# Attention and two MLPs on one core: an earlier start, a lower rank and a longer planned landing for the second MLP's weight narrowing

## The chip, the core and the metric

The kernel runs on one core of a Trainium2 chip. The metric is the device time of one execution in microseconds (us); of the kernel before there are three runs, and their median stands below. One further execution was taken with the hardware profiler, and all rows come from that one.

## The reference

```python
# attention with a window of 64 over 4 batches, 8 heads, 576 positions, 64 per head
scores = scale * np.matmul(q, k.transpose(0, 1, 3, 2))
scores = np.where((rel >= 0) & (rel < 64), scores, -1000000000.0)
attn = softmax(scores); x = attn @ v        # 2304 tokens x 512
# first MLP, 512 -> 2048 -> 512
h = x @ w_in
x = (h * (1.0 / (1.0 + np.exp(-1.702 * h)))) @ w_out
# second MLP, 512 -> 1536 -> 512
xn = x / np.sqrt(np.mean(x * x, axis=-1, keepdims=True) + 1e-06) * rms_g
g = xn @ w_gate
out = (g * (1.0 / (1.0 + np.exp(-g))) * (xn @ w_val)) @ w_out
```

All five weight matrices arrive as float64, so every weight is narrowed to float32 on the chip from its bits, and the products are made of a high and a low part of each operand (three matmuls for one).

## The kernel before, in words

**Stages.** The tokens are cut into 36 groups of 64 for the attention and into six blocks of 512, 256 and four times 384 tokens for the first MLP. The first eight groups are done at the start. Then the first MLP runs as 96 steps, 16 for each block (step s = 16 x block + column): 12 matmuls of an up-projection (L554 to L556), a gate on ScalarE and VectorE (L607, L611, L312, L569), and two steps later 12 matmuls of a down-projection (L628 to L630). The attention of the next block's groups runs beside the steps. When a block is finished, its sums of squares go through a small chain of DMAs to DRAM and back: `ms` (L706), `ss` (L697), a root on GpSimd (L693), and the store `rs` (L700) of four-byte words. After step 95 the second MLP runs on three blocks of 768 tokens (L912 to L914, L1013 to L1015).

**One round of attention.** Scores (L428, TensorE), mask and highest (L453, L458, VectorE), powers (L463, ScalarE), reciprocal (L468, L469, VectorE), normalisation (L472, GpSimd), a turn of the tile (L477 on TensorE up to the second block; after it L520 on VectorE with some ten small moves into the tile `pts` on ScalarE and GpSimd, L312 and L314), then the values (L487, TensorE). The loads are `q` (L398), `k` (L405) and `v` (L413), all on SP's queue. The tiles `q` and `k` have two buffers; `v` has one, so that the load for the next round is issued only after L487 of this one.

**Narrowing a second-MLP weight.** There are 36 of them (12 tiles each of gate, value and out). `b_narrow` calls `w_narrow`, which loads 512 KB of float64 into one of three `raw` buffers (L336, SP), scales the high words (L340, ScalarE), and shifts, joins and signs on VectorE (L344, L348, L354). For a pair of gate or value tiles four sums follow (L1172, VectorE or GpSimd), and each half of the pair is stored to DRAM (`wp`, L1175, 512 KB); its buffer is free for the next raw load only when that store has landed. An out tile is signed into a `y` buffer, so its raw buffer is free at once, and it is stored with L1158 (`wr`). The second MLP later reads these stores back (`fw`, L865, and L898).

**What sets the order.** Nothing of this order is decided on the chip. `Planner` holds every operation with a cost, its dependencies and a rank (`prio`), and `emit` plays the program through in planned time: of the operations that are ready, the one with the lowest rank number goes first, and each engine's instructions are then written out in that order. Each engine, SP's queue among them, runs its list strictly in order. A DMA counts as landed a planned 2.2 us after its transfer, plus `late`:

```python
if best == "D" or o.late:
    o.end += self.DMA_WAIT + o.late
```

So `late` costs no time on the chip by itself: it only makes the planner place what uses the data further back. Weight i of the 36 is planned around step `p = n0 + i * (n1 - n0) / 36`, and its load is not issued before the up-projection of step p - 2.

Of the kernel before, what the change touches and what calls it, by code (L numbers as in the profile page):

```python
# [11 lines left out]
I32 = mybir.dt.int32  # L12
# [5 lines left out]
P = 128  # L18
# [171 lines left out]
def act(n, sbuf=True, extra=0):  # L190
    return n / 1200.0 + (0.093 if sbuf else 0.05) + 0.093 * extra


def dve(n, fast=False):
    return n * (0.52e-3 if fast else 1.042e-3) + 0.068


def pool(n):
    return n * 2.4e-3 + 0.16


def dma(nbytes):
    return max(nbytes / 320e3, 0.45)
# [3 lines left out]
def window_attention_two_moe_kernel(ctx: ExitStack, tc: tile.TileContext, ins, out):  # L207
    nc = tc.nc
# [14 lines left out]
    NBA = len(sizes)  # L223
# [66 lines left out]
    pl = Planner({k: v[1] for k, v in KINDS.items()})  # L290
# [5 lines left out]
    def make(b):  # L296
        if b.kind == "pt":
            b.tile = pts
            return pts
        if b.kind == "xa":  # L300
            turn = xa_turn[0] = 1 - xa_turn[0]
            b.tile = words(SUMS)[:, turn * 512:(turn + 1) * 512].rearrange("p (k c) -> p k c", k=NK)
            return b.tile
        p, n, shape, dt = KINDS[b.kind]
        b.tile = p.tile(shape, b.dt or dt, tag=b.kind, name=b.kind, bufs=n)
        return b.tile
# [21 lines left out]

    w32 = {}

    def w_narrow(key, src, prio, after=(), apart=False):
        rb = Buf("raw")
        fb = Buf("y") if apart else rb

        def fetch(e):
            nc.sync.dma_start(out=make(rb), in_=src.bitcast(I32).rearrange("p (n two) -> p n two", two=2))  # L336

        def scaled(e):
            high = rb.tile[:, :, 1].bitcast(F32)
            nc.scalar.activation(out=high, in_=high, func=AF.Copy, scale=2.0 ** -112)  # L340

        def shifted(e):
            low = rb.tile[:, :, 0]
            nc.vector.tensor_scalar(out=low, in0=low, scalar1=29, scalar2=None, op0=ALU.logical_shift_right)  # L344

        def joined(e):
            low, high = rb.tile[:, :, 0], rb.tile[:, :, 1]
            nc.vector.scalar_tensor_tensor(  # L348
                out=low, in0=high, scalar=3, in1=low, op0=ALU.logical_shift_left, op1=ALU.bitwise_or)

        def signed(e):
            low, high = rb.tile[:, :, 0], rb.tile[:, :, 1]
            to = make(fb).bitcast(I32) if apart else high
            nc.vector.scalar_tensor_tensor(  # L354
                out=to, in0=high, scalar=-2147483648, in1=low, op0=ALU.bitwise_and, op1=ALU.bitwise_or)

        got = pl.op({"D": dma(P * 4096)}, fetch, prio - 3, new=[rb], after=after, late=5.0 if apart else 0.0)
        pl.op({"A": act(512)}, scaled, prio, w=[rb])
        pl.op({"V": dve(512, True)}, shifted, prio, w=[(rb, "low")], after=[got], port="V")
        pl.op({"V": dve(512)}, joined, prio, w=[rb], r=[(rb, "low")], port="V")  # L360
        if apart:
            pl.op({"V": dve(512)}, signed, prio, r=[rb, "at"], new=[fb], port="V")
        else:
            pl.op({"V": dve(512)}, signed, prio, r=["at"], w=[rb], port="V")
        w32[key] = fb
# [235 lines left out]
    def a_up(j, c, prio):  # L601
        n = sizes[j]
        hb, o = up("h", lambda: slab_of(2 * c), ("slab", 2 * c), tok0[j], n, prio)
        tb = Buf("th")

        def squash(e):
            nc.scalar.activation(out=make(tb)[:, 0:n], in_=hb.tile[:, 0:n], func=AF.Tanh, scale=0.851)  # L607

        def gated(e):
            th = tb.tile[:, 0:n]  # L610
            nc.vector.scalar_tensor_tensor(out=th, in0=th, scalar=1.0, in1=hb.tile[:, 0:n],  # L611
                                           op0=ALU.add, op1=ALU.mult)

        pl.op({"A": act(n, False)}, squash, prio, r=[hb], new=[tb])
        pl.op({"V": dve(n)}, gated, prio, r=[hb], w=[tb])
        return split(tb, n, prio, tok0[j]), o
# [128 lines left out]
    def both(n, alone=False):  # L745
        return {"V": dve(n)} if alone else {"G": pool(n), "V": dve(n)}
# [96 lines left out]
    w32p_d = [dr_p.tile([P, 2, 512, 2], F32, name=f"wp{n}") for n in range(NU)]  # L843
    w32o_d = [dr_p.tile([P, 512], F32, name=f"wr{c}") for c in range(NB)]
# [238 lines left out]
    for g in range(NS):  # L1083
        late = g >= 2
# [13 lines left out]
    first, need = {}, {}  # L1098
# [7 lines left out]
    for i in order:  # L1106
        c = i // 2
        key, src = (("in", c), w_in[c]) if i % 2 == 0 else (("out", c), w_out[c])
        prio = need[i] - LEAD if need[i] > 0 else -57.5
        w_narrow(key, src, prio)  # L1110
        w_split(key, i, prio)
# [10 lines left out]
    ups = []  # L1122
# [15 lines left out]
        b_list.append((("v", c), w_val[c], c - c % 2 + 1))  # L1138
        b_list.append((("o", c), w_o2[c], c + 2))
    b_list.sort(key=lambda x: x[2])  # L1140
    n0, n1 = first[2] + 2, first[NBA - 1] - 4

    def ex_open(e):
        actx.close()
# [6 lines left out]
    def b_narrow(i):  # L1151
        (kind, c), src, _ = b_list[i]
        p = n0 + i * (n1 - n0) / len(b_list)
        key = ("w32d", "o", c) if kind == "o" else ("w32d", c - c % 2 + "gv".index(kind), c % 2)
        w_narrow(key, src, p + 3, after=[ups[int(p) - 2]], apart=kind == "o")
        b = w32.pop(key)
        if kind == "o":
            pl.op({"D": dma(P * 2048)}, lambda e: nc.sync.dma_start(out=w32o_d[c], in_=b.tile), p + 3, r=[b], w=[key])  # L1158
            return
        n = key[1]  # L1160
        if c % 2 == 0:
            halfway[n] = b
            return
        pair = (halfway.pop(n), b)

        def word(h, k, lane):
            return pair[h].tile[:, k * 256:(k + 1) * 256, lane].bitcast(F32)

        for to, x, y, op in (((0, 0), (1, 0, 1), (1, 1, 1), ALU.add), ((0, 1), (0, 0, 0), (0, 0, 1), ALU.subtract),
                             ((1, 0), (0, 0, 1), (1, 0, 1), ALU.subtract), ((1, 1), (0, 1, 1), (0, 1, 0), ALU.subtract)):  # L1170
            xs = [(n, "sum", *v[:2]) for v in (x, y) if v[2] == 0]
            fn = lambda e, to=to, x=x, y=y, op=op: eng[e].tensor_tensor(out=word(*to, 0), in0=word(*x), in1=word(*y), op=op)  # L1172
            pl.op(both(256), fn, p + 3, r=[*pair, *xs], w=[(n, "sum", *to)], port="GV")
        for h in range(2):
            pl.op({"D": dma(P * 4096)}, lambda e, h=h: nc.sync.dma_start(  # L1175
                out=w32p_d[n][:, h].bitcast(I32), in_=pair[h].tile), p + 3,
                r=[pair[h], (n, "sum", h, 0), (n, "sum", h, 1)], w=[("w32d", n, h)])

    plans.sort()
# [2 lines left out]
    for s in range(SA):  # L1182
        j, c = steps[s]
        while pi < len(plans) and plans[pi][0] <= s:
            p, g = plans[pi]
            pi += 1
            load_q(g, p - 4)
            load_k(g, p - 4)
            load_v(g, p - 3)
            attention(g, p - 0.3, 2)  # L1190
        gs, o = a_up(j, c, s)
        ups.append(o)
        gates[s] = gs
        if s - 2 in gates:
            a_down(s - 2)
        while bi < len(b_list) and n0 + bi * (n1 - n0) / len(b_list) <= s:
            b_narrow(bi)
            bi += 1
# [78 lines left out]
```

## Time and profile before

| | |
|---|---|
| median of three runs | 937.48 us (937.11 to 937.95) |
| the profiled execution's own time | 937.76 us |
| its span in the profile | 936.0 us |
| PE (TensorE matmul) busy | 909.0 us, 97% of the span |
| DVE (VectorE) busy | 648.8 us, 69% |
| ACT (ScalarE) busy | 436.4 us, 47% |
| POOL (GpSimd) busy | 275.3 us, 29% |
| mean DMA rate | 208 GB/s |

PE is busy nearly all the time, so the question for any change is what it does to the 27 us in which PE is not, and to the stretches in which PE runs at a lower granted clock. The busy times of the other engines are averages over stages and say little about one stage.

### The profile page before, as it was taken

Reading aid. Unit: us, or ns where it says so; the run is one execution under the profiler, and the core shown is the slowest. Engines: PE = TensorE matmul, PEld = TensorE weight load, DVE = VectorE, ACT = ScalarE, POOL = GpSimd, SP = SyncE. Lnnn points to the kernel's source line nnn. Section 1 sums busy time; section 2 is a strip of 40 time slices with the busy share of each in tenths; the row PEclk is TensorE's granted clock in tenths of the full one; section 3 lists DMA queues with packets and bytes.
Section 4 is the critical chain, followed back from the end, with each engine's and each line's share of the span. In section 5 each row is a group of like instructions: output and inputs, shape, how many; then the busy total and the mean of one; then the engine's idle time right before and its main releaser. Section 6 shows DMA issues by size and latency. Waiting matters only on the chain.

```text
span 936.0 us, 15370 instructions
## 1 busy us (share of the span) xinstructions
PE 909.0 (97%) x5436; PEld 843.1 (90%) x5436; DVE 648.8 (69%) x1237; ACT 436.4 (47%) x1078; POOL 275.3 (29%) x389
## 2 busy tenths in 40 slices
PE   8899999998999999999999999999999999999998
PEld 7787789988899999989999889998999999999997
DVE  5999974465777677675367888878767556555553
ACT  6666664464566567456336534454322224322222
POOL 4111021132345345333012633334223225222210
PEclk9899999999899999999999999999999999999999
DMA  8756532348666566753565999977987677976651
GB/s 274 237 182 203 175 121 56 109 139 192 224 220 205 180 228 240 184 205 122 68 236 172 302 280 332 369 277 246 319 247 209 204 204 235 291 204 205 203 153 67
DMA packets 86536, 194.63 MB, mean 208 GB/s; under 512 B 12726, under 2 KB 36027, under 8 KB 84924
## 3 DMA queue, kind: packets, MB, share of 16 engines
q1 hardware_dynamic: 66108, 137.02, 45.4%
q0 software_dynamic: 20352, 56.63, 20.5%
q8 instruction: 43, 0.70, 0.3%
q14 instruction: 33, 0.27, 0.1%
HBM read 140.13 MB, written 53.50 MB: 207 GB/s over the span
## 4 chain that ended last, share of the span: by engine, by line
PE 69%; DVE 13%; DMA 9%; issue 3%; ACT 3%; POOL 1%; SPq 1%; DVEq 0%; ACTq 0%; POOLq 0%
PE bank L912 8%; PE bank L913 8%; PE bank L914 8%; PE y L628 4%; PE y L630 4%; PE y L629 4%; PE bank L555 4%; PE bank L554 4%; PE bank L556 4%; PE y L1013 3%; PE y L1015 3%; PE y L1014 3%; DMA wp<-raw 3%; DVE raw L348 3%; PE abank L428 2%
## 5 line engine op out<-in xcount | busy, mean ns | idle before, releaser
L554 PE MATMUL bank<-xh,slab 128*128 128x384 f32 (+2 forms) x288 | 99.6, 346 | 0.8 <-DVE th L611 0.8
L556 PE MATMUL bank<-xh,slab 128*128 128x384 f32 (+2 forms) x288 | 97.5, 339 | 1.9 <-DVE slab L381 1.9
L628 PE MATMUL y<-gh,slab 128*128 128x384 f32 (+2 forms) x288 | 98.4, 342 | 0.0
L555 PE MATMUL bank<-xl,slab 128*128 128x384 f32 (+2 forms) x288 | 97.7, 339 | 0.5 <-DVE xl L494 0.5
L630 PE MATMUL y<-gh,slab 128*128 128x384 f32 (+2 forms) x288 | 96.9, 336 | 0.0
L629 PE MATMUL y<-gl,slab 128*128 128x384 f32 (+2 forms) x288 | 96.9, 336 | 0.0
L951 ACT ACTIVATE sb<-gh 128x384 f32<-128x384 f32 x72 | 37.8, 525 | 113.6 <-DVE gh L938 113.5
L312 ACT ACTIVATE xh<-sb 128x384 fp32r<-128x384 f32 x72 | 37.1, 521 | 105.9 <-DVE sb L966 105.9
L938 DVE TENSOR_TENSOR gh<-gl,bank 128x384 f32<-128x384 f32 x108 | 59.3, 551 | 37.3 <-PE bank L914 36.8
L611 DVE SCALAR_TENSOR_TENSOR th<-th,bank 128x384 f32<-128x384 f32 (+2 forms) x96 | 52.6, 547 | 44.9 <-ACT th L607 44.8
L913 PE MATMUL bank<-slab,late 128*128 128x384 f32 x228 | 77.1, 338 | 0.0
L913 PE MATMUL bank<-slab,slab 128*128 128x384 f32 x228 | 76.5, 335 | 0.0
L607 ACT ACTIVATE th<-bank 128x384 f32<-128x384 f32 (+2 forms) x96 | 46.4, 483 | 59.1 <-PE bank L556 53.4
L472 POOL TENSOR_TENSOR e<-e,rc 128x512 f32<-128x512 f32 x34 | 37.0, 1087 | 121.4 <-DVE rc L469 97.5
L312 ACT ACTIVATE gh<-th 128x384 fp32r<-128x384 f32 (+2 forms) x96 | 50.2, 524 | 43.6 <-DVE th L611 40.2
L938 DVE TENSOR_TENSOR gl<-gl,bank 128x384 f32<-128x384 f32 x72 | 39.8, 553 | 35.7 <-PE bank L914 32.1
L340 ACT ACTIVATE raw<-raw 128x512 f32<-128x512 f32 x68 | 46.1, 682 | 29.3 <-DMA raw<-in_w_gate_dram 11.0
L569 DVE TENSOR_TENSOR gl<-th,gh 128x384 fp32r<-128x384 f32 (+2 forms) x74 | 44.5, 601 | 21.1 <-ACT gh L312 20.6
L556 PEld LDWEIGHTS bank<-xh,slab 128*128 128x128 f32 x288 | 54.5, 189 | 4.8 <-DVE slab L381 2.7
L463 ACT ACTIVATE e<-e,nm 128x128 f32<-128x128 f32 x112 | 43.6, 391 | 32.0 <-DVE nm L458 31.9
L554 PEld LDWEIGHTS bank<-xh,slab 128*128 128x128 f32 x288 | 54.7, 190 | 3.7 <-DVE th L611 1.8
L555 PEld LDWEIGHTS bank<-xl,slab 128*128 128x128 f32 x288 | 54.7, 190 | 2.9 <-DVE xl L494 0.9
(197 smaller groups left out, 2631.2 us busy)
## 6 DMA issues: line engine op xcount, KB each, us to landing
slab<-wc POOLq DMA_DIRECT2D x36, 512.0 KB, 4.8
late<-wc POOLq DMA_DIRECT2D x36, 512.0 KB, 4.2
wp<-raw SPq DMA_DIRECT2D x24, 512.0 KB, 2.7
fw<-wp SPq DMA_DIRECT2D x12, 1024.0 KB, 11.4
late<-wo POOLq DMA_DIRECT2D x22, 512.0 KB, 5.5
q<-in_q_dram SPq DMA_DIRECT2D x36, 256.0 KB, 4.8
wc<-slab SPq DMA_DIRECT2D x18, 512.0 KB, 7.3
wc<-late SPq DMA_DIRECT2D x18, 512.0 KB, 6.1
```

What stands on the lines that cost most here:

```text
L312: nc.scalar.activation(out=out, in_=in_, func=AF.Copy)
L554: nc.tensor.matmul(h, w[:, 0, kk], xh_ring[:, kk, cols], start=(kk == 0), stop=False)
L555: nc.tensor.matmul(h, w[:, 0, kk], xl_ring[:, kk, cols], start=False, stop=False)
L556: nc.tensor.matmul(h, w[:, 1, kk], xh_ring[:, kk, cols], start=False, stop=(kk == NK - 1))
L611: nc.vector.scalar_tensor_tensor(out=th, in0=th, scalar=1.0, in1=hb.tile[:, 0:n], op0=ALU.add, op1=ALU.mult)
L628: nc.tensor.matmul(y, s[:, 0, cols], hb.tile[:, 0:n], start=first, stop=False)
L629: nc.tensor.matmul(y, s[:, 0, cols], lb.tile[:, 0:n], start=False, stop=False)
L630: nc.tensor.matmul(y, s[:, 1, cols], hb.tile[:, 0:n], start=False, stop=last)
L912: nc.tensor.matmul(h, w[:, 0, kk], xh[:, kk], start=kk == 0, stop=False)
L913: nc.tensor.matmul(h, w[:, 0, kk], xl[:, kk], start=False, stop=False)
L914: nc.tensor.matmul(h, w[:, 1, kk], xh[:, kk], start=False, stop=kk == 1)
L938: nc.vector.tensor_tensor(out=(make(to) if kind else s.tile)[:, 0:HT].bitcast(F32), in0=s.tile[:, 0:HT].bitcast(F32), in1=b.tile[:, 0:HT], ...
```

## The change

Four things, all in the planner's input for the 36 narrowings of the second MLP's weights:

1. Every raw load of a second-MLP weight gets `late=6.0`. Before, the out tiles had 5.0 and the gate and value tiles had nothing. First-MLP weights keep none.
2. `n0` goes from step 34 to step 16, the first step of the second token block; `n1` stays at step 76. The 36 narrowings are spaced 1.67 steps apart instead of 1.17.
3. The ranks go from p + 3 to p + 8 (the load's from p to p + 5), for the narrowing, the sums and the stores.
4. The load's earliest moment stays at the up-projection of step p - 2, with the new p.

No instruction is added or removed: the change moves them.

```diff
-    def w_narrow(key, src, prio, after=(), apart=False):
+    def w_narrow(key, src, prio, after=(), apart=False, late=0.0):
...
-        got = pl.op({"D": dma(P * 4096)}, fetch, prio - 3, new=[rb], after=after, late=5.0 if apart else 0.0)
+        got = pl.op({"D": dma(P * 4096)}, fetch, prio - 3, new=[rb], after=after, late=late)
...
-    n0, n1 = first[2] + 2, first[NBA - 1] - 4
+    n0, n1 = first[1], first[NBA - 1] - 4
...
-        w_narrow(key, src, p + 3, after=[ups[int(p) - 2]], apart=kind == "o")
+        w_narrow(key, src, p + 8, after=[ups[int(p) - 2]], apart=kind == "o", late=6.0)
...
-            pl.op({"D": dma(P * 2048)}, lambda e: nc.sync.dma_start(out=w32o_d[c], in_=b.tile), p + 3, r=[b], w=[key])
+            pl.op({"D": dma(P * 2048)}, lambda e: nc.sync.dma_start(out=w32o_d[c], in_=b.tile), p + 8, r=[b], w=[key])
...
-            pl.op(both(256), fn, p + 3, r=[*pair, *xs], w=[(n, "sum", *to)], port="GV")
+            pl.op(both(256), fn, p + 8, r=[*pair, *xs], w=[(n, "sum", *to)], port="GV")
...
-                out=w32p_d[n][:, h].bitcast(I32), in_=pair[h].tile), p + 3,
+                out=w32p_d[n][:, h].bitcast(I32), in_=pair[h].tile), p + 8,
```

Three places in the order of instructions.

**VectorE, the fourth narrowing (the second value tile), before.** It stands in the third token block (384 columns); L344 is the first instruction on VectorE that needs the raw load.

```order
L520 STREAM_TRANSPOSE t_2634<-e 128x512
L611 SCALAR_TENSOR_TENSOR th<-th,bank 128x384
L569 TENSOR_TENSOR gl<-th,gh 128x384
L344 TENSOR_SCALAR raw<-raw 128x512
L348 SCALAR_TENSOR_TENSOR raw<-raw 128x512
L611 SCALAR_TENSOR_TENSOR th<-th,bank 128x384
L354 SCALAR_TENSOR_TENSOR raw<-raw 128x512
L494 TENSOR_TENSOR xl<-abank,xh 128x4x64
L453 SCALAR_TENSOR_TENSOR e<-abank,m_rest 128x512
```

**The same narrowing in the changed kernel.** The second L344 is that of the fifth (an out tile); the turn of the attention tile (L314) stands behind both.

```order
L469 RECIPROCAL rc<-rc 128x4
L611 SCALAR_TENSOR_TENSOR th<-th,bank 128x256
L344 TENSOR_SCALAR raw<-raw 128x512
L569 TENSOR_TENSOR gl<-th,gh 128x256
L348 SCALAR_TENSOR_TENSOR raw<-raw 128x512
L344 TENSOR_SCALAR raw<-raw 128x512
L314 COPY pts<-abank 128x512
L611 SCALAR_TENSOR_TENSOR th<-th,bank 128x256
L354 SCALAR_TENSOR_TENSOR raw<-raw 128x512
```

It has moved from the third block into the second. Between its load on SP's queue and its L344 there is now at least one whole round of attention; before there was none.

**SP's queue at the end of the first token block, before** (`ms`, `ss`, `rs` as above; `v`, `q`, `k` are the loads of the rounds that follow):

```order
L706 DMA ms_119<-sq 1x512
L413 DMA v<-in_v_dram 128x512
L398 DMA q<-in_q_dram 128x512
L697 DMA ss<-ms_119 128x4x1
L405 DMA k<-in_k_dram 128x512
L700 DMA rs_125<-ss 128x4x1
L413 DMA v<-in_v_dram 128x512
L398 DMA q<-in_q_dram 128x512
```

**The same place in the changed kernel:**

```order
L1175 DMA wp_131<-raw 128x1024
L706 DMA ms_119<-sq 1x512
L1175 DMA wp_131<-raw 128x1024
L413 DMA v<-in_v_dram 128x512
L697 DMA ss<-ms_119 128x4x1
L398 DMA q<-in_q_dram 128x512
L405 DMA k<-in_k_dram 128x512
L336 DMA raw<-in_w_val_dram 128x1024
L700 DMA rs_125<-ss 128x4x1
L336 DMA raw<-in_w_o_dram 128x1024
L413 DMA v<-in_v_dram 128x512
L398 DMA q<-in_q_dram 128x512
```

Four transfers of 512 KB are new here, and one of them (the raw load of an out tile) stands between the store `rs` and the next load of `v`.

**TensorE, the second of the attention rounds in the second token block, before** (L554 to L556 up-projection, L628 to L630 down-projection, twelve matmuls each):

```order
L630 MATMUL y_1678<-gh,slab_93 128x256
L487 MATMUL abank<-pts,v 64x64 x8
L428 MATMUL abank<-k,q 128x128 x4
L554 MATMUL bank<-xh,slab_98 128x256
L555 MATMUL bank<-xl,slab_98 128x256
```

**and in the changed kernel:**

```order
L556 MATMUL bank<-xh,slab_96 128x256
L487 MATMUL abank<-pts,v 64x64 x8
L428 MATMUL abank<-k,q 128x128 x4
L628 MATMUL y_1648<-gh,slab_93 128x256
L629 MATMUL y_1648<-gl,slab_93 128x256
```

The values and the scores of this and the next three rounds stand one down-projection (12 matmuls) earlier in TensorE's list.

## Rows read from the trace of the kernel before

**Rows 1.** Windows by stage: length, busy PE, PEld, DVE, ACT, POOL, PEclk, DMA, GB/s.
```profile
128.00:194.00 66.00, 64.47 (x583) 61.60 (x582) 31.61 (x71) 34.02 (x107) 13.04 (x14) 1.00 0.32 91
194.00:440.00 246.00, 237.49 (x1578) 229.58 (x1578) 174.75 (x337) 147.13 (x433) 99.76 (x166) 0.98 0.63 198
440.00:506.00 66.00, 66.00 (x380) 65.61 (x378) 39.03 (x70) 28.62 (x56) 9.85 (x7) 1.00 0.51 133
```

**Rows 2.** Waits of PE from 194 to 240 us: total, times, longest.
```profile
PE abank L487 <- POOL pts L314: 4.7, 2, 4.0
```

**Rows 3.** Window around 400 us (columns as in Rows 1).
```profile
396.50:402.00 5.50, 2.84 (x17) 2.32 (x18) 5.19 (x11) 3.77 (x11) 4.53 (x7) 1.00 0.61 216
```

**Rows 4.** The chain that ended last, 205 to 236 and 378 to 398 us: start, length.
```profile
210.21 11.05 DMA wp<-raw
221.28 3.54 DMA raw<-in_w_val_dram
...
381.89 9.99 DMA wp<-raw
```

**Rows 5.** Groups of DVE by line: busy, mean ns, idle before and releasers.
```profile
L348 DVE SCALAR_TENSOR_TENSOR raw<-raw 128x512 int32<-128x512 int32 x68 | 51.9, 764 | 4.1 <-ACT raw L340 3.0
L344 DVE TENSOR_SCALAR raw<-raw 128x512 int32<-128x512 int32 x68 | 29.9, 439 | 16.4 <-DMA raw<-in_w_gate_dram 8.8 <-DMA raw<-in_w_val_dram 5.8 <-DMA raw<-in_w_in_dram 0.9
```

**Rows 6.** Timeline of SP's queue, 206 to 226 us: start and length of one issue.
```profile
209.22 0.39 SPq L700 DMA_DIRECT2D rs<-ss  x1
```

**Rows 7.** Windows after the two waits of PE (columns as in Rows 1).
```profile
234.90:241.70 6.80, 5.63 (x32) 5.36 (x33) 5.01 (x9) 4.22 (x12) 2.38 (x5) 0.50 0.84 281
402.15:405.55 3.40, 3.40 (x25) 3.28 (x22) 2.30 (x5) 1.83 (x4) 1.00 (x1) 0.50 0.65 234
```

**Rows 8.** Timelines of PE and ACT: two rounds of attention in the third block.
```profile
253.72 1.05 PE L428 MATMUL abank<-k,q 128*128 128x128 f32 x7
265.23 0.69 PE L487 MATMUL abank<-pts,v 128*64 128x64 f32 x16
277.31 1.16 PE L428 MATMUL abank<-k,q 128*128 128x128 f32 x8
287.98 1.92 ACT L312 ACTIVATE pts<-t 32x128 f32<-32x128 f32 x6
```

**Rows 9.** Waits of PE from 128 to 194 us.
```profile
PE abank L477 <- POOL e L472: 0.8, 1, 0.8
PE abank L487 <- ACT pts L312: 0.7, 1, 0.7
```

**Rows 10.** Timeline of SP's queue at the first block's end.
```profile
152.24 0.38 SPq L700 DMA_DIRECT2D rs<-ss  x1
157.27 0.33 SPq L413 DMA_DIRECT2D v<-in_v_dram  x1
```

**Rows 11.** Windows after that store (columns as in Rows 1).
```profile
153.00:159.00 6.00, 6.00 (x64) 5.80 (x63) 2.27 (x5) 2.03 (x5) 0.23 (x1) 1.00 0.07 3
163.00:166.40 3.40, 3.40 (x41) 3.20 (x40) 0.95 (x3) 1.63 (x4) 0.41 (x1) 1.00 0.69 207
```

**Rows 12.** DMA issues from 150 to 170 us: KB each, median us to landing.
```profile
v<-in_v_dram SPq DMA_DIRECT2D x2, 256.0 KB, 8.2
```

**Rows 13.** Timeline of PE: the turn and the values of one round, second block.
```profile
163.76 0.60 PE L477 MATMUL abank<-ident,e 128*128 128x128 f32 x4
165.71 0.69 PE L487 MATMUL abank<-pts,v 128*64 128x64 f32 x16
```

**Rows 14.** Last narrowing's signing, first load of the second MLP, its landing, its use.
```profile
436.07 0.68 DVE L354 SCALAR_TENSOR_TENSOR y<-raw 128x512 int32<-128x512 int32 x1
...
454.00 1.18 SPq L865 DMA_DIRECT2D fw<-wp  x1
...
fw<-wp SPq DMA_DIRECT2D x1, 1024.0 KB, 13.4
...
473.09 0.66 ACT L312 ACTIVATE slab<-fw 128x512 fp32r<-128x512 f32 x1
```

## The prediction

> **What bounds the kernel now.** I read the busy time by stage first, then the waits of TensorE (PE), then the chain of waits behind the long ones, and last the single queues. The windows by stage [rows 1] show PE busy 237.5 of 246 us from 194 to 440 us, where the second MLP's weights are narrowed, at a mean granted clock of 0.98, against 1.00 in the stages around it. VectorE (DVE) is far from full: 174.8 of 246 us there, 31.6 of 66 us in the stage before. So only PE's own gaps and its slow stretches can be won or lost.
>
> PE's gaps in the narrowing stage come in two clusters. From 194 to 240 us it waits 4.0 + 0.7 us for the values of one round of attention [rows 2]; from 396.5 to 402 us it is busy 2.84 of 5.5 us, a gap of 2.7 us [rows 3]. That leaves 8.5 - 4.7 - 2.7 = 1.1 us of small waits. The chain that ended last shows what is behind both clusters [rows 4]: a store `wp` of a summed half, 11.05 and 9.99 us long, then the raw load that had to wait for its buffer, 3.54 us the first time. DVE stands 5.8 us at L344 for the first of these loads [rows 5], and all that is behind L344 in its list (mask, highest, reciprocal of the round) is late with it. The store is slow for a reason that SP's queue shows [rows 6]: it went out 1 us behind the store `rs` of four-byte words. Each cluster is followed by a stretch at half clock [rows 7], the lower of the two levels (1.2 instead of 2.4 GHz), of 6.8 and 3.4 us. All of DVE's L344 waits sum to 16.4 us [rows 5], but only these two clusters reach PE with more than a microsecond.
>
> **What the change takes away.** Both clusters, as I read the orders. Counted there, 13 of the 36 L344 stood behind their load by less than one round of attention; in the changed kernel it is one, at the very start. A store and a load took 11.05 + 3.54 = 14.6 us at worst; a round takes 265.23 - 253.72 = 11.5 us [rows 8], and between load and L344 there is now one round and part of another. The sum:
> - first cluster: 4.7 us of waiting, and 6.8 us at half speed, which cost 3.4 us;
> - second cluster: 2.7 us of waiting, and 3.4 us at half speed, which cost 1.7 us.
>
> Together 12.5 us. The low end is the second cluster alone, 4.4 us, if the first comes back at another `rs` store; the high end is 13.6 us, with the small waits, which I leave where they are.
>
> **What it moves.** Eight narrowings now stand in the second token block. Each costs DVE 0.44 + 0.76 us [rows 5] and 0.76 us for L354, of L348's form, 1.96 us together, so 15.7 us on top of 31.6 in a stage of 66 [rows 1]: covered by idle time. What lies on a path is the block's last round: three raw instructions (1.96 us) now stand in DVE's list between its highest and its reciprocal, and the sums of a pair. The 0.8 + 0.7 us that PE waits there [rows 9] could grow by a microsecond, but the round also starts twelve matmuls sooner. I take nothing for it, with 1 us either way.
>
> **What it adds: a wait at the first block's end.** After its `rs` store at 152.24 us [rows 10] the queue is nearly dead: 3 GB/s up to 159 us, and 207 GB/s only from 163 us on [rows 11]. The load of `v` behind it, issued at 157.27 us, lands 8.2 us later, at 165.5 us [rows 10, 12]. The values that need it start at 165.71 us [rows 13], so the cover is 0.2 us. Two things of the change use it up. In PE's list these values move twelve matmuls earlier: from the turn to the values there are 1.95 us, of which 0.60 us are the turn [rows 13], so about 1.4 us; PE wants `v` at 164.3 us. And a raw load of 512 KB now stands between `rs` and `v`. At the 207 GB/s of the row it takes 2.5 us; if it moves wholly in the dead time, nothing. The wait is thus between 165.5 - 164.3 = 1.2 us and 3.7 us, or 4.7 us if `rs` itself goes out a microsecond later behind the two new `wp` stores. I take 3.0 us, nearer the upper end, since the dead time moves almost nothing. A cluster of 2.7 us was followed by 3.4 us at half clock, one of 4.7 us by 6.8 us [rows 7]; one of 1.5 us, at 190 us, was not, as the clock of 1.00 around it tells [rows 1, 9]. So I add 1.7 us: **4.7 us in all**, between 1.2 and 4.7 + 3.4 = 8.1 us. The other `rs` stores have most of a round or more between them and the next use of a `v` behind them; I count nothing there.
>
> **The tail.** The last narrowing's signing, at 436.07 us [rows 14], moves five gates (L611) further back in DVE's list, 5 x 66 / 16 = 20.6 us in that stage [rows 1], to about 457 us. The second MLP's buffers can be opened only then. Its first weights' load, now issued at 454.00 us and landed 13.4 us later, at 467.4 us, is used at 473.09 us [rows 14]. I expect it to go out some 4 us later and to land at about 471.5 us: still hidden, by 1.5 us. If that cover goes, ScalarE is late by what is missing, and PE feels it only beyond the two steps that it has ahead. No price.
>
> **The sum.** 937.76 us, the profiled execution's own time, less 12.5, plus 4.7, is 930.0 us. The median of the runs is 0.3 us below that execution, so I say **929.7 us**. About 0.2% (1.9 us) is what a measurement of this kernel can tell from no change.
>
> **Rivals.**
> - *No new wait at the first block's end.* `v` lands in time, and the gain stays whole: 937.5 - 12.5 = 925.0 us. For it: `rs` may go out as before while the raw load finds its room in the dead time, and half of what I price is clock, which a short gap would not touch. Against it: the cover is 0.2 us, and PE asks 1.4 us sooner. Chance 0.20. The Trainium skill's page "DMA: Bandwidth & Descriptors", section "Anatomy of one DMA — SWDGE (gpsimd) path", would give this result: it fits the time of a DMA as 2.0 us plus its bytes at 436 GB/s, an estimate of 2.6 us for `v`, well before PE wants it. The 8.2 us of the row behind an `rs` store do not agree with that fit.
> - *The waits only move; the change does not do what it says.* The planned 6 us are no more than a number if real stores take 10 us: in the third block a pair of `wp` stores again stands right behind an `rs`, and one triple of raw loads meets the same wait, 4.7 + 3.4 = 8.1 us. Time: 937.5 - 12.5 + 8.1 + 4.7 = 937.8 us, no change. For it: the `rs` stores are as many as before and as slow. Against it: the distance from load to L344 has grown by about a round nearly everywhere. Chance 0.15.
> - *Slower: the rounds become too tight.* With the raw loads believed to be safe, the planner sets nearly every round's values five up-projections behind its scores, 11.5 us as in [rows 8], where several rounds had six before. A round with raw instructions between its links took from 277.31 to 287.98 + 1.92 = 289.90 us, 12.6 us [rows 8]. Nine of the rounds from the third block on carry three narrowings each. If each makes PE wait 1.5 us, that is 13.5 us, and the time is 937.5 - 12.5 + 4.7 + 13.5 = 943.2 us. It decides from the point where such rounds take over 11.5 us; above 0.9 us a round the gain is gone. Against it: PE's small waits of today are 1.1 us in all, with many rounds of this length, and the long rounds stood beside loads that came late. Chance 0.12.
>
> The forecast keeps 0.53.
>
> **How the numbers follow.** Faster by over 0.2% are the forecast and the first rival, 0.73; within 0.2% is the second, 0.15; slower the third, 0.12. The range reaches down to the first rival with the small waits gone too, 925.0 - 1.1 = 923.9 us, and up to the second, 937.8 us. It leaves out the third and little else. The bounds of the new wait (1.2 to 8.1 us) give 926.2 to 933.1 us and lie inside it.
>
> **What the profile would show.** Right: no wait of PE for L487 over 1 us from 194 to 440 us, the clock at 1.00 there, L344's idle time on raw loads under 3 us, and one new gap of 2 to 4 us at L487 near 164 us, behind a load of `v`, with a short stretch at half clock after it. The forecast is wrong where `v` lands early (first rival), where a `wp` or raw load of about 10 us again ends in L344 and L487 (second), or where PE waits a microsecond for `pts` in round after round, with nothing late on the queue (third).

## The result, and the profile after

The changed kernel takes 925.19 us (median of 4 runs, 924.56 to 926.32) against 937.72 us for the kernel before on the same chip (4 runs): a ratio of 0.9862, 95% interval 0.9839 to 0.9885, faster by 12.5 us or 1.3%. On a second chip it was 928.49 against 943.02 us, ratio 0.984 (0.9806 to 0.9874). The kernels below ran on several chips, on which the kernel before took 937.7 to 944.9 us, so each is compared by its ratio to the kernel before on its own chip.

The forecast was 929.7 us. The sign and the range held; the result is that of the first rival, 925.0 us. The profiled execution took 925.49 us with a span of 923.7 us, 12.3 us shorter than before.

The stages after (length, busy PE, PEld, DVE, ACT, POOL, PEclk, DMA share, GB/s), against [rows 1]:

```profile
0.00:128.00 128.00, 118.13 (x720) 94.84 (x721) 112.92 (x223) 82.63 (x211) 22.11 (x32) 0.99 0.63 211
128.00:194.00 66.00, 64.35 (x566) 60.99 (x564) 47.88 (x97) 37.39 (x112) 18.74 (x20) 1.00 0.62 185
194.00:440.00 246.00, 245.36 (x1674) 238.84 (x1675) 162.28 (x315) 153.54 (x447) 99.66 (x164) 1.00 0.52 174
440.00:506.00 66.00, 64.14 (x365) 63.24 (x364) 40.26 (x77) 28.82 (x55) 9.47 (x9) 1.00 0.56 188
506.00:660.00 154.00, 150.48 (x778) 138.00 (x778) 126.51 (x222) 67.96 (x130) 57.70 (x59) 1.00 0.91 300
```

From 194 to 440 us PE now stands still for 0.64 us in place of 8.5 us, and the granted clock is 1.00 in place of 0.98. The second block carries the moved narrowings: DVE 47.88 us in place of 31.61, and PE lost nothing by it (64.35 against 64.47 us).

The windows in which the clock was at half [rows 7], after:

```profile
234.90:241.70 6.80, 6.80 (x43) 6.80 (x42) 6.24 (x12) 4.25 (x14) 1.70 (x2) 1.00 0.36 119
402.15:405.55 3.40, 3.40 (x22) 3.40 (x21) 2.41 (x7) 2.10 (x10) 1.11 (x2) 1.00 0.76 300
```

All waits of PE from 194 to 440 us that the view lists (total, times, longest), where [rows 2] had 4.7 us at L487 alone up to 240 us:

```profile
PE bank L554 <- DVE th L611: 0.5, 1, 0.5
PE abank L487 <- ACT pts L312: 0.4, 1, 0.4
```

DVE's group of the shift, which had 16.4 us of idle time before it [rows 5]; both releasers left are weights of the first MLP:

```profile
L344 DVE TENSOR_SCALAR raw<-raw 128x512 int32<-128x512 int32 x68 | 33.3, 494 | 2.2 <-DMA raw<-in_w_out_dram 1.2 <-DMA raw<-in_w_in_dram 0.9
```

SP's queue at the second block's end, where the first cluster of waits used to begin (start, length of the issue); nothing is issued between these two lines:

```profile
210.23 0.38 SPq L700 DMA_DIRECT2D rs<-ss  x1
218.19 1.85 SPq L1175 DMA_DIRECT2D wp<-raw  x2
```

The two stages of the kernel before that [rows 1] leaves out, for comparison (first the start, then 506 to 660 us):

```profile
0.00:128.00 128.00, 119.75 (x727) 98.27 (x728) 113.50 (x223) 83.43 (x212) 23.14 (x32) 0.97 0.62 208
506.00:660.00 154.00, 149.33 (x770) 136.48 (x771) 122.99 (x211) 69.30 (x134) 61.34 (x60) 1.00 0.90 302
```

So the 12.3 us come from two places. The narrowing stage gives 8.5 - 0.6 = 7.9 us of waiting and (6.8 + 3.4) / 2 = 5.1 us of clock, 13.0 us in all. The other stages together take back 0.7 us: from the rows above and those of before, PE's idle time grows by 1.6 us up to 128 us and by 1.9 us from 440 to 506 us, and shrinks by 1.2 us after that, while 3.4 us less at half clock in the first stage give 1.7 us.

At the first block's end, where the forecast saw a new wait, there is none. SP's queue there (start, length of the issue):

```profile
149.66 0.42 SPq L405 DMA_DIRECT2D k<-in_k_dram  x1
150.17 0.38 SPq L336 DMA_DIRECT2D raw<-in_w_val_dram  x1
152.34 0.38 SPq L700 DMA_DIRECT2D rs<-ss  x1
152.77 0.50 SPq L336 DMA_DIRECT2D raw<-in_w_o_dram  x1
157.40 0.33 SPq L413 DMA_DIRECT2D v<-in_v_dram  x1
```

The landing of this `v` (DMA issues, 150 to 166 us: KB, us from issue to landing):

```profile
v<-in_v_dram SPq DMA_DIRECT2D x1, 256.0 KB, 6.8
```

The values on PE:

```profile
165.88 0.69 PE L487 MATMUL abank<-pts,v 128*64 128x64 f32 x16
```

`v` lands at 157.40 + 6.8 = 164.2 us and the values start at 165.88 us: 1.7 us of cover, although a raw load of 512 KB stands between `rs` and `v`. (In a second trace of the same kernel, that of the third call below, `v` took 7.8 us and the cover was 0.7 us: still no wait.) The windows behind the store show how the load got through (a share above 1 comes about because a packet's whole time is counted where it starts):

```profile
152.00:154.00 2.00, 2.00 (x19) 2.00 (x18) 0.36 (x3) 1.36 (x6) 1.06 (x2) 1.00 1.05 411
154.00:156.00 2.00, 2.00 (x20) 2.00 (x19) 1.18 (x3) 1.01 (x2) 0.30 (x1) 1.00 1.98 251
156.00:158.00 2.00, 2.00 (x29) 1.80 (x28) 0.60 (x2) 0.98 (x3) 0.00 (x0) 1.00 0.94 16
158.00:160.00 2.00, 2.00 (x20) 2.00 (x19) 1.62 (x3) 0.12 (x1) 0.74 (x1) 1.00 0.21 26
```

Which load this was is told by the bytes, from 149 to 154 us and from 154 to 156 us:

```profile
DMA packets 1165, 1.30 MB, mean 260 GB/s; under 512 B 656, under 2 KB 656, under 8 KB 1165
DMA packets 602, 0.50 MB, mean 251 GB/s; under 512 B 480, under 2 KB 480, under 8 KB 602
```

The four loads issued from 148.19 us up to `rs` (`v`, `q`, `k` and a raw load) are 1.31 MB, so the 411 GB/s are still theirs. The raw load behind `rs` (0.52 MB) follows at 251 GB/s, beside the small pieces of `rs`, and only then comes the dead time. In it the DMA engines count as busy (a share of 0.94) and move next to nothing (16 GB/s).

### The profile page after: what moved, and what is told of

Read it like the earlier page. It is cut to its first block, busy times and chain, and to the rows that moved or that the text cites. A ratio compares the mean times of both kernels' runs of the same rounds, so it can differ in the third digit from the quotient of the medians.

```text
span 923.7 us, 15362 instructions
## 1 busy us (share of the span) xinstructions
PE 902.2 (98%) x5436; PEld 835.9 (90%) x5436; DVE 647.3 (70%) x1236; ACT 438.4 (47%) x1081; POOL 273.2 (30%) x387
## 4 chain that ended last, share of the span: by engine, by line
PE 77%; DVE 12%; DMA 6%; issue 2%; ACT 2%; SPq 0%; POOL 0%; DVEq 0%; ACTq 0%; POOLq 0%
PE bank L912 9%; PE bank L913 9%; PE bank L914 9%; PE y L628 5%; PE y L630 5%; PE y L629 5%; PE bank L554 5%; PE bank L555 5%; PE bank L556 5%; PE y L1013 3%; PE y L1015 3%; PE y L1014 3%; PE abank L428 3%; DVE raw L348 2%; PE abank L487 2%
## 5 line engine op out<-in xcount | busy, mean ns | idle before, releaser
L554 PE MATMUL bank<-xh,slab 128*128 128x384 f32 (+2 forms) x288 | 98.3, 341 | 1.0 <-DVE th L611 1.0
L628 PE MATMUL y<-gh,slab 128*128 128x384 f32 (+2 forms) x288 | 98.5, 342 | 0.5 <-DVE y L653 0.5
L556 PE MATMUL bank<-xh,slab 128*128 128x384 f32 (+2 forms) x288 | 97.0, 337 | 2.0 <-DVE slab L381 2.0
L630 PE MATMUL y<-gh,slab 128*128 128x384 f32 (+2 forms) x288 | 96.9, 337 | 0.5 <-DVE slab L381 0.5
L913 PE MATMUL bank<-slab,slab 128*128 128x384 f32 x228 | 76.4, 335 | 0.0
L556 PEld LDWEIGHTS bank<-xh,slab 128*128 128x128 f32 x288 | 54.1, 188 | 4.9 <-DVE slab L381 2.8
L554 PEld LDWEIGHTS bank<-xh,slab 128*128 128x128 f32 x288 | 54.1, 188 | 3.6 <-DVE th L611 1.6
L630 PEld LDWEIGHTS y<-gh,slab 128*128 128x128 f32 x288 | 54.1, 188 | 3.2 <-DVE slab L381 1.2
L912 PE MATMUL bank<-slab,slab 128*128 128x384 f32 x156 | 53.0, 340 | 3.8 <-ACT th L312 1.7
```

Source lines behind the costliest of these rows:

```text
L554: nc.tensor.matmul(h, w[:, 0, kk], xh_ring[:, kk, cols], start=(kk == 0), stop=False)
L556: nc.tensor.matmul(h, w[:, 1, kk], xh_ring[:, kk, cols], start=False, stop=(kk == NK - 1))
L628: nc.tensor.matmul(y, s[:, 0, cols], hb.tile[:, 0:n], start=first, stop=False)
L630: nc.tensor.matmul(y, s[:, 1, cols], hb.tile[:, 0:n], start=False, stop=last)
L912: nc.tensor.matmul(h, w[:, 0, kk], xh[:, kk], start=kk == 0, stop=False)
L913: nc.tensor.matmul(h, w[:, 0, kk], xl[:, kk], start=False, stop=False)
```

## The experiments

**First call: the parts one at a time.** Theory D (distance) was mine: all that counts is that a round of attention stands between a raw load and its L344, so the planned landing alone should do it. Theory S gives the credit to the early start, theory R to the rank.

*The planned landing alone.*

```diff
-        got = pl.op({"D": dma(P * 4096)}, fetch, prio - 3, new=[rb], after=after, late=5.0 if apart else 0.0)
+        got = pl.op({"D": dma(P * 4096)}, fetch, prio - 3, new=[rb], after=after, late=late)
...
-        w_narrow(key, src, p + 3, after=[ups[int(p) - 2]], apart=kind == "o")
+        w_narrow(key, src, p + 3, after=[ups[int(p) - 2]], apart=kind == "o", late=6.0)
```

> The kernel before with the planned landing of 6 us alone (start of the narrowings and ranks as before). Theory D (distance: what counts is only that a round of attention stands between a raw load and its L344): both clusters of waits go, 937.7 - 12.5 = 925 us, between 924 and 928; L344 stands under 3 us for raw loads. Theory S (the early start, which takes 8 of 36 narrowings out of the full third to fifth blocks): no more than a third of the gain, 934 us or above. Theory R (the lower rank lets attention go first): 935 us or above.

Measured: 968.19 against 942.91 us, ratio 1.0231 (1.0198 to 1.0265): slower by 25 us. Theories S and R foretold no gain, but no theory a loss. Theory D is right about L344, which does not stand at all for raw loads of the second MLP. But the kernel loses elsewhere. Two of its stages:

```profile
194.00:440.00 246.00, 229.34 (x1509) 220.24 (x1509) 164.82 (x325) 139.49 (x408) 79.40 (x137) 0.97 0.56 178
440.00:506.00 66.00, 51.15 (x297) 48.81 (x296) 27.72 (x56) 25.62 (x62) 10.07 (x16) 0.90 0.48 126
```

PE's longest wait from 440 to 500 us is 12.7 us; the group from 128 to 500 us (total, times, longest):

```profile
PE y L628 <- ACT y L650: 14.9, 4, 12.7
```

The chain that ended last there (start, length):

```profile
469.83 11.52 DMA xn<-y
481.44 0.59 ACT y L650
```

Longer planned distances make every raw buffer turn over more slowly. With the start left at step 34 the last L344 comes at 466 us, beside the end of the fifth block. The block's evictions (L650, L653) share the two `y` buffers with the out tiles, and the store `xn` that would free one went out at 469.83 us, right behind an `rs` store at 469.41 us. It took 11.5 us, and PE waited 12.7 us. The rest, 16.7 us of idle time from 194 to 440 us against 8.5, is spread over many small waits for evictions and gates; which of them comes from what was not taken apart.

*The early start alone, and the rank alone.*

```diff
-    n0, n1 = first[2] + 2, first[NBA - 1] - 4
+    n0, n1 = first[1], first[NBA - 1] - 4
```

> The kernel before with the early start alone (step 16 in place of 34; no planned landing for gate and value tiles, ranks as before). Theory D: 17 of the 36 L344 stand within a round of their load, so stores wp behind an rs store again hold a raw load and L344 with it: 934 to 941 us, no gain over 0.4%. Theory S: most of the gain, 925 to 929 us. Theory R: 935 us or above.

```diff
-        w_narrow(key, src, p + 3, after=[ups[int(p) - 2]], apart=kind == "o")
+        w_narrow(key, src, p + 8, after=[ups[int(p) - 2]], apart=kind == "o")
```

(and p + 8 for the sums and both stores)

> The kernel before with the ranks at p + 8 alone. Theory D: 16 of the 36 L344 stand within a round of their load: 934 to 941 us, L344 stands 10 us or more for raw loads. Theory R: most of the gain, 925 to 929 us. Theory S: as before, 936 to 939 us.

Measured: 952.42 us for the start, ratio 1.009 (1.0063 to 1.0118), and 945.23 us for the rank, ratio 1.0011 (0.9992 to 1.003). Neither gains anything, as theory D said, and the start alone costs more than the range it was given. SP's queue with the early start alone:

```profile
153.08 0.38 SPq L700 DMA_DIRECT2D rs<-ss  x1
153.68 2.26 SPq L1175 DMA_DIRECT2D wp<-raw  x2
163.09 0.33 SPq L336 DMA_DIRECT2D raw<-in_w_gate_dram  x1
```

PE's wait from 160 to 176 us:

```profile
PE abank L477 <- POOL e L472: 6.5, 1, 6.5
```

The window behind it, at half clock:

```profile
168.20:174.90 6.70, 3.71 (x18) 3.48 (x20) 4.37 (x10) 2.67 (x5) 1.04 (x1) 0.50 0.81 292
```

This is the first cluster of before again, now at another `rs`: two `wp` stores right behind it, a raw load that has to wait 9.4 us for their buffer, and L344 in the way of a round. With the rank alone the cluster stays where it was: a `wp` of 11.48 us behind the `rs` at 212.44 us, and two waits of PE, 4.1 and 2.7 us.

*Start and rank without the planned landing* (the changed kernel, less this line):

```diff
-        w_narrow(key, src, p + 8, after=[ups[int(p) - 2]], apart=kind == "o", late=6.0)
+        w_narrow(key, src, p + 8, after=[ups[int(p) - 2]], apart=kind == "o")
```

(the out tiles at 5.0 as before)

> The changed kernel without the planned landing (early start and lower rank kept, the out tiles at 5 us as before). Theory D: the gain goes, 934 to 941 us, with waits of PE for pts of over 2 us somewhere from 130 to 440 us. Theories S and R: 925 to 929 us, as the changed kernel.

Measured: 947.66 us, ratio 1.0031 (1.0 to 1.0062). The gain is gone, as theory D expected, with a wait of 7.0 us at L477 at 166 us and one of 4.9 us at L487 at 313 us. So the planned landing is needed, and is not enough.

**Second call: the landing with one other part, the queue, and the price of a load.** Theory M (room) came from the first call: the landing does the work, the early start gives it the room that it costs, the rank is a detail.

*Landing and start, without the rank* (the changed kernel with p + 3 in all four places):

```diff
-        w_narrow(key, src, p + 8, after=[ups[int(p) - 2]], apart=kind == "o", late=6.0)
+        w_narrow(key, src, p + 3, after=[ups[int(p) - 2]], apart=kind == "o", late=6.0)
```

> The changed kernel with the ranks back at p + 3 (planned landing and early start kept). Theory M (the planned landing keeps the loads off the path, the early start gives the three raw buffers the room that this costs, the rank is a detail): as the changed kernel, 1.0 to 1.6% faster than before, L344 under 3 us on raw loads, no wait of PE over 2 us from 130 to 440 us. Theory R (with the higher rank the triples of narrowings go ahead of the links of a round and of the gates): within 0.5% of before or slower, with waits of PE for gates or pts of 1 to 3 us.

Measured: 936.35 us, ratio 0.9916 (0.9886 to 0.9945): somewhat over half of the gain, less than theory M asked for and more than theory R allowed, so the rank is more than a detail. The longest wait left is one of 1.6 us at 237 us, with 6.8 us at half clock behind it, and its chain is the known one:

```profile
216.84 13.90 DMA wp<-raw
230.81 5.74 DMA raw<-in_w_o_dram
```

This fits a distance that does what it was planned for: a store and a load of 19.6 us together cost a wait of 1.6 us, where 14.6 us had cost 4.7 us before.

*Landing and rank, without the early start* (the changed kernel with this line as before):

```diff
-    n0, n1 = first[1], first[NBA - 1] - 4
+    n0, n1 = first[2] + 2, first[NBA - 1] - 4
```

> The changed kernel with the start back at step 34 (planned landing and lower rank kept). Theory M: the triples, each some 21 us apart, have no room before the fifth block's end, so it is slower than before by 1.5 to 3%, with a wait of PE of 5 us or more near that end. Theory R: the rank mends what the planned landing alone did, 1.0 to 1.6% faster than before.

Measured: 955.03 us, ratio 1.0114 (1.0077 to 1.0152). Slower, by a little less than theory M asked for, so the rank does not mend what the landing alone did. The waits are only in part where theory M put them: 4.2 us at L487 at 438 us, and 6.7 us at L912 at 675 us, in the second MLP. How the second one comes from the order was not followed further.

*The small store on another queue* (the kernel before; the trace has six of these stores, one for each block, not five):

```diff
-            nc.sync.dma_start(out=rs_d[j].rearrange("one (t p) -> p (one t)", p=P), in_=cb.tile[:, 0:n // P])
+            nc.scalar.dma_start(out=rs_d[j].rearrange("one (t p) -> p (one t)", p=P), in_=cb.tile[:, 0:n // P])
```

> The kernel before with the five small stores rs on ScalarE's queue, nothing else changed. Theory Q (what stands behind rs is slow because it shares SP's queue with it): the stores wp near 210 us land in under 5 us, the first cluster of waits is gone, 0.5 to 1.0% faster than before. Theory E (the dead time lies in what the queues share): wp still takes 9 us or more, within 0.3% of before, or slower where ScalarE stands for the issue.

Measured: 943.21 us, ratio 0.9988 (0.9959 to 1.0016), and the chain behind the store, which now went out on ScalarE's queue at 209.55 us:

```profile
211.44 12.31 DMA wp<-raw
223.76 4.38 DMA raw<-in_w_val_dram
```

Theory E holds: the store `wp` is as slow as before [rows 4] though the small store is no longer on its queue. That fits what the Trainium skill says of queues in general ("DMA: Bandwidth & Descriptors", section "Issuing engines are not separate DMA queues"): transfers of all issuing engines run on the same 16 DMA engines.

*One load between `rs` and `v`* (the kernel before, with a load into a raw buffer that nothing reads):

```diff
             nc.sync.dma_start(out=rs_d[j].rearrange("one (t p) -> p (one t)", p=P), in_=cb.tile[:, 0:n // P])
+            if j == 0:
+                for i in range(1):
+                    spare = at.tile([P, 512, 2], I32, tag="raw", name="raw", bufs=3)
+                    nc.sync.dma_start(out=spare, in_=w_gate[i].bitcast(I32).rearrange("p (n two) -> p n two", two=2))
```

> The kernel before with one spare load of 512 KB into a raw buffer that nobody reads, issued right behind the first rs store and ahead of the next load of v; the place of the values in PE's list stays as before. By the price of my prediction (2.5 us at 207 GB/s after the dead time) v lands near 168 us and PE waits 2 us or more at L487 near 166 us. By the rival (the load moves before the dead time begins) v lands at 165.5 us or earlier, and PE waits less than 0.5 us there.

Measured in one run: 951.28 us, where the kernel before had a median of 944.86. PE's wait at that place:

```profile
PE abank L487 <- DMA v<-in_v_dram: 3.5, 1, 3.5
```

The window behind it:

```profile
169.20:176.00 6.80, 5.75 (x38) 5.66 (x39) 1.80 (x3) 1.70 (x7) 0.73 (x1) 0.50 0.38 116
```

So a load that stands there alone does cost what the prediction feared, and more than the 4.7 us that it took: `v` landed 11.8 us after its issue at 158.27 us, and 3.5 us of waiting and 6.8 us at half clock make 6.9 us, inside the bounds of 1.2 to 8.1 us. What differs in the changed kernel is seen in the packets from 152 to 156 us, first of the changed kernel, then of this one:

```profile
DMA packets 974, 1.32 MB, mean 331 GB/s; under 512 B 575, under 2 KB 575, under 8 KB 974
```

```profile
DMA packets 561, 0.08 MB, mean 19 GB/s; under 512 B 536, under 2 KB 536, under 8 KB 561
```

Both moved the small pieces of `rs`. But beside them the changed kernel moved 974 - 575 = 399 large packets, this one 25. In the changed kernel a `k` load and a raw load had been issued 2 us ahead of `rs` and were still moving, and the load behind it followed them; here what had been issued ahead had landed, and the load was caught. The two kernels differ in more than this, and that the transfers in flight decide it was not tried by itself. As a rule it does not hold: in the kernel without the rank the third `rs` went out at 306.05 us with loads still moving (332 GB/s from 306 to 307 us), and the raw load issued 0.42 us behind it took 13.0 us all the same:

```profile
raw<-in_w_o_dram SPq DMA_DIRECT2D x1, 512.0 KB, 13.0
```

Whether the amount in flight decides, or something else, stays open.

**Third call: the cause itself.** If every cluster is something that was caught behind an `rs` store, the store is the thing to change. Theory N says that the dead time comes from the number of four-byte writes, theory S (not that of the first call) that any store in pieces this small brings it on.

*The changed kernel again*, for the same chip:

> The changed kernel once more, as a measure for the other three on the same chip: 1.1 to 1.6% faster than before, no wait of PE over 1 us from 128 to 440 us.

Measured: 928.49 against 943.02 us, ratio 0.984 (0.9806 to 0.9874); one wait of 1.5 us is left (L554, at 201 us).

*The start in the middle* (the changed kernel):

```diff
-    n0, n1 = first[1], first[NBA - 1] - 4
+    n0, n1 = first[1] + 9, first[NBA - 1] - 4
```

> The changed kernel with the start of the narrowings at step 25 in place of 16 (34 before). Theory M (room: twelve triples, each some 21 to 26 us behind the one before, must end before the fifth block's sums): from step 25 on there are 51 steps, some 215 us, for what took 12 x 21.5 = 258 us with the start at step 34, so part of the gain goes: 0 to 0.9% faster than before, with waits of PE for gates or evictions between 350 and 450 us. Rival theory (only the first rs store, at the end of the first block, and the few narrowings beside the second block count): as the changed kernel, 1.1 to 1.6% faster.

Measured: 936.62 us, ratio 0.9901 (0.9867 to 0.9934). The size lies between the two theories, and the interval reaches into the range of each. The reason of theory M is not seen: from 350 to 450 us there are one wait of 1.5 us, behind a `v` load, and one of 1.0 us, and nothing shows that room is missing. About one half of what is lost is lost at the first `rs` store; SP's queue there:

```profile
153.09 0.38 SPq L700 DMA_DIRECT2D rs<-ss  x1
153.52 0.50 SPq L336 DMA_DIRECT2D raw<-in_w_gate_dram  x1
158.07 0.33 SPq L413 DMA_DIRECT2D v<-in_v_dram  x1
```

PE's long waits from 160 to 200 us:

```profile
PE abank L487 <- DMA v<-in_v_dram: 4.1, 1, 4.1
PE abank L477 <- POOL e L472: 2.5, 1, 2.5
```

The packets from 152 to 156 us:

```profile
DMA packets 560, 0.08 MB, mean 19 GB/s; under 512 B 536, under 2 KB 536, under 8 KB 560
```

Here the wait that I had predicted for the change does occur, with a raw load alone behind `rs`: 4.1 us of waiting and 3.4 us at half clock behind it. The other half is the wait of 2.5 us at 197 us, with 6.8 us at half clock behind it; no `rs` store stands near it, and its cause was not followed. So theory M is down to this: an early enough start is needed, and beyond that the time depends in good part on what happens to stand next to the `rs` stores.

*Fewer, longer pieces in the kernel before.* In `ss` and `rs` a partition now holds tokens that lie next to each other, 128 pieces of 8 to 16 bytes in place of 256 to 512 of four; no instruction moves.

```diff
-            nc.sync.dma_start(out=make(cb)[:, 0:n // P], in_=ms_d[j].rearrange("one (t p) -> p (one t)", p=P))
+            nc.sync.dma_start(out=make(cb)[:, 0:n // P], in_=ms_d[j].rearrange("one (p t) -> p (one t)", p=P))
...
-            nc.sync.dma_start(out=rs_d[j].rearrange("one (t p) -> p (one t)", p=P), in_=cb.tile[:, 0:n // P])
+            nc.sync.dma_start(out=rs_d[j].rearrange("one (p t) -> p (one t)", p=P), in_=cb.tile[:, 0:n // P])
```

> The kernel before, its order of instructions untouched; only the addresses of the small transfers ss and rs change, so that a partition holds n/128 tokens that lie next to each other (128 pieces of 8 to 16 bytes in place of 256 to 512 of four). Theory N (the dead time comes from the number of four-byte writes): the stores wp near 210 us land in under 5 us, the first cluster goes, 0.5 to 1.2% faster than before. Theory S (any store in pieces this small brings it on): wp still takes 9 us or more, within 0.3% of before.

Measured: 923.47 us, ratio 0.9784 (0.9748 to 0.9819): 2.2% faster than the kernel before with its order untouched, and the fastest kernel of this study, 5 us below the changed kernel on this chip (the intervals just meet). The narrowing stage:

```profile
194.00:440.00 246.00, 244.73 (x1650) 237.57 (x1648) 179.41 (x348) 155.12 (x448) 99.90 (x167) 1.00 0.60 200
```

The chain behind the second `rs`:

```profile
208.67 6.85 DMA wp<-raw
215.53 3.47 DMA raw<-in_w_val_dram
```

`wp` takes 6.85 us in place of 11.05 (I had said under 5), and that is enough: PE stands still for 1.27 us in the stage in place of 8.5, at a clock of 1.00, and L344's idle time is 6.6 us in place of 16.4. `v` behind the first `rs` lands in 3.4 us in place of 8.2 [rows 12]. The gain is larger than theory N foretold, but it holds in its main point. `ss` and `rs` were changed together, and no run changes one alone, but the traces point to `rs`. The store of the second block, from issue to landing, in the kernel before and then here:

```profile
rs<-ss SPq DMA_DIRECT2D x1, 1.0 KB, 9.6
rs<-ss SPq DMA_DIRECT2D x1, 1.0 KB, 4.3
```

The loads `ss` did not become shorter (3.3 and 3.7 us for the third and fourth block before, 3.8 and 4.7 us here). The number of pieces and their length change together, so which of the two counts is not told apart.

The Trainium skill ("DMA: Bandwidth & Descriptors", section "Specifications") puts the size from which a transfer runs at line rate at 512 bytes, with a read-modify-write below it. The trace agrees that such a store is slow: 9.6 us for 1 KB. But by that line alone 8 to 16 bytes would be as bad as four, and the runs show that a half to a quarter of the pieces already frees the path; pieces of 512 bytes were not tried.

*The same addresses in the changed kernel* (the same two lines):

> The changed kernel with the same new addresses of ss and rs. Theory N: the dead times are shorter, but no wait of PE from 128 to 440 us is left for them to take away, so within 0.3% of the changed kernel on this chip. Theory S: the same time, with the dead times as they were. A gain over 0.3% would say that a dead time still cost something in the changed kernel.

Measured: 926.2 us, ratio 0.9803 (0.9771 to 0.9835), 2.3 us or 0.25% below the changed kernel on this chip, with intervals that overlap, as theory N expected. Both ways of taking the clusters away win the same time once; they don't add.

## Why the prediction was right, and where it was wrong

- **What the change takes away: right in size, and in part for another reason.** 12.5 us foretold for the two clusters; the stage gave 13.0 us, the difference being the small waits that I had left in place. Both clusters went, with the clock behind them, and L344 no longer stands on second-MLP loads. The kernel without the landing shows that the landing is needed (947.66 us, with other clusters). But I had expected slow stores and loads that the distance covers, and here they are not slow, since nothing stands right behind the second, third and fourth `rs`. At the second block's end `wp` used to follow `rs` within 1 us [rows 4, 6]; now the next issue comes 8.0 us later, as the queue above shows, and behind the third and the fourth `rs` 5.2 us later. I had not foreseen that the planner's order would come out so; this part is luck. That the distance also helps where a store is slow is suggested by the kernel without the rank (1.6 us of waiting behind 19.6 us), and was not tried by itself.
- **What it adds: the step that failed.** I priced a new wait at the first block's end at 4.7 us, bounds 1.2 to 8.1; it measured nothing. It had two halves. In the first I let PE ask for `v` 1.4 us sooner and kept the landing of `v` where it was. But `v` has one buffer, so its load goes out when the values of the round before are done, and these stand twelve matmuls earlier too: from the issue to the values there are 165.71 - 157.27 = 8.44 us before and 165.88 - 157.40 = 8.48 us after. That neither time has moved by 1.4 us is mostly chance: PE comes to the sums of the first block (L685) at 145.10 us in place of 143.59, and 0.9 us of these 1.5 us were there at 128 us, behind a stage that the change hardly touches. The second half, the load between `rs` and `v`, was priced too low rather than too high for a load that stands there alone (6.9 us), but the load of the change is not alone, and its bytes moved ahead of the dead time; `v` landed in 6.8 us in place of 8.2. I had put the queue's order into the section on the change, with `q`, `k` and a raw load ahead of `rs`, and then priced only what stands behind it. I had also read the 3 GB/s of [rows 11] as a queue held for six microseconds; up to 157.27 us there was nothing issued for it to move [rows 10], and the DMA share of 0.07 there is that of an idle queue, unlike the 0.94 above.
- **What it moves: right.** DVE took 16.3 us more in the second block, PE 0.1 us less.
- **The tail: that it has no price was right, its times were wrong.** The last signing came at 442.4 us, not at 457, since I had added five gates and forgotten that the gain brings them all forward by 12 us (436 + 20.6 - 12.5 = 444). The first load of the second MLP went out at 445.0 us and was used at 458.5 us; PE's idle time up to 506 us is 1.9 us.
- **The first rival (no new wait, 925.0 us) is what happened**, in part for the reason given for it: the raw load found its room. The room was ahead of the dead time, not in it. That its time agrees to 0.2 us is luck: the other stages took back 0.7 us, and the first of them alone varies by more than that. The fit that it quotes from the Trainium skill is, as its section's title says, for transfers issued by GpSimd; `v` goes out on SP's queue, and its 6.8 us do not agree with that fit's estimate of 2.6 us either.
- **The second rival (waits only move) fell for this change**, but is what most of the variants did: the same dead time caught `wp`, `xn` or `v` at other `rs` stores.
- **The third rival (tight rounds) fell.** No wait of PE over 0.5 us is left from 194 to 440 us.

The theory with which I went to the chip, that the distance from load to L344 is the whole matter, fell with the first run (25 us slower). What stands is that the landing, an early enough start and the rank together give an order in which nothing that is needed soon is caught behind an `rs` store. The kernel with other addresses shows that the small transfers `ss` and `rs` are the cause, and the landing times of `rs` point to the store of the two; the order is a way around it.

## What to carry to other kernels

When a large transfer is late time after time, look at what was issued just before it: here it was, time and again, a store of 1 to 2 KB in four-byte pieces, and changing two address patterns won at least as much as a new order of the whole program. To price a transfer behind such a store, read the queue on both sides of it: with loads still in flight ahead one load got through and another was held, so such a price needs wide bounds. Parts of a planner's change don't add up; of this one, each part alone gained nothing or lost, up to 25 us.

## What the runs showed that I had not expected

- The dead time behind a store of four-byte pieces follows it onto another queue (`wp` 12.3 us with the store on ScalarE's queue, 11.1 us on SP's) and shrinks with fewer, longer pieces (6.85 us with half as many, of twice the size). The store itself lands sooner too, after 4.3 us in place of 9.6.
- A load issued 0.4 us behind such a store moved at 251 GB/s beside its pieces when other loads had been in flight, and was held when there were none (19 GB/s over the same 4 us, other traffic included); at another `rs` store it was held although loads were in flight.
- PE was busy for 115.65 to 119.99 us of the first 128 us over the traces, though the changes hardly touch that stage: a spread of 4 us, a third of the gain. Stages have to be compared, not totals.
